# The order of score tiles at unit boundaries, and the join to the output projection, in a fused attention-times-gate kernel

## The chip, the cores and the metric

One core of one Trainium2 chip runs the whole kernel in one launch. The metric is the device time of that launch in microseconds (us), lower is better.

## What is computed

```python
xn = layernorm(x)                                    # x: 2048 x 512
q, k, v = split heads of (xn @ wqkv)                 # 32 heads of 16
o = softmax(q @ k.T * 16 ** -0.5) @ v                # per head, 2048 x 2048
s = o.reshape(2048, 512) @ wo
g = silu(gelu(xn @ w1 + b1) @ w2 + b2)               # hidden size 1376
out = x + s * g
```

All operands are float32. Products that need the precision are made of three matmuls on rounded high parts and remainders (`mm3`: high x high, high x low, low x high).

## The kernel before

The first stages (to about 437 us) make the layer norm, q, k, v and the gate g, and write q, k and g to DRAM. Among them the first 588 *score tiles* are already made (`SOON`). The rest, which the change touches, is the attention.

**Units and steps.** A unit is four heads by 512 queries; there are 32 (`NU`), and a unit takes 16 steps, one for each 128 keys. Steps are counted by n; `ua, ka = divmod(n, 16)` names the unit and the step in it, written (u, k) below. `L` is 512. A step is written out by hand as a string of letters, and each engine runs its own instructions in the order in which the letters issue them:

- **T** (`t_one`, L760): one *transposed tile*, 128 keys by 512 queries of one head, on half of the array's rows (contraction over 48 rows of q parts and 2 rows that hold the negated maxima, high and low). Four T make a step; the second and third share the two-bank tile `two`, the first writes a `ps` bank, the fourth `pst`. ScalarE turns them into exponentials (L763, L765): three ACTIVATEs a step.
- **S** (`s_whole`, L212): one *score tile*, 128 queries by 512 keys of one head, of which VectorE takes the maximum over keys (`s_max`, L218). Its only use is the row maximum that a later unit's T needs.
- **X, Y**: one score tile made in two halves of 256 columns, X on the upper rows and Y on the lower, with one maximum after Y. Y stands behind a no-op that waits until X is done. A step's usual string is `XTSTTYSTV` (three score tiles), or `TSTTSTV` (two).
- **V** (`pv_step`, L832): probabilities of the step before times v, with a column of ones for the denominator; four column tiles of 17 columns, accumulated over 16 steps in one PSUM bank. After the 16th, VectorE copies the bank out (`os`, L839).
- **H** (`w_halves`, L960): a quarter of one side of the output projection of two token tiles, six matmuls on half rows.
- **W** (`w_out`): gate and residual of a finished token tile, and its write to DRAM.

**Banks.** Score tiles rotate over three banks (`s_ring`). For units 1 to `FEW` the step (u, 1) makes two score tiles instead of three, and V changes its bank with the ring there. Units above `FEW` keep V's bank, so V of (u, 0), issued in step (u, 1), must wait for the copy of the unit before; there all steps make three score tiles, and step (u, 0) has the order `FIRST`.

**Maxima.** When a unit's 64 score tiles are done, `s_end0` reduces them to `nm`, `s_turn` transposes (L263) and splits them on GpSimd (`mh`, L265 and L266), and some steps later `s_send` writes them to DRAM (`mh_d`, L296; for the last unit two of the four writes come from GpSimd's queue, two from SyncE's). `load_mh` reads them back into the q tile's rows (L182) before the unit's first T.

**The join.** From step `DONE` on, no score tile is left. Steps then carry H, in the orders of `TWO` and `BOTH`, and two steps' V stand together in every second step. `gate` computes tanh on ScalarE (L894) and a product on VectorE (L895); `w_two` rounds two tiles of o to high parts on ScalarE (L938) and remainders on GpSimd (L941). `at(n, f, ...)` puts such helpers into step n, by default behind its fourth T (pos=3).

**The end.** After step 512 come the last six token tiles: three matmuls per k block (L107, in `mm3`), `w_gate` (L966), `w_add` (L971) and the write (L972). The last tile is done in two halves of 256 columns (`cols`).

Of the kernel before, what the change touches and what calls it, by code (L numbers as in the profile page):

```python
# [16 lines left out]
P = 128  # L17
S = 2048
D = 512
H = 32  # L20
DH = 16
KT = D // P
NT = S // P
# [11 lines left out]
NW = 10  # L35
EARLY = 4
AHEAD = ((-3, 0), (-3, 3), (-2, 0), (-2, 3))
DONE = 493
FILL0 = 2
APART = 5  # L40
HB = 5
DEALT = "00111111121112121112121112121112111211111212111212111212111212111211"
W2B = 2
ORDER = {0: "TTTTV", 2: "TSTTSTV", 3: "XTSTTYSTV"}
FIRST = "STXTTSYTV"
TWO = ("HTTTTHWV", "TTTTHHV")
BOTH = {DONE: "HHTTTTV", DONE + 3: "HHTTTTWV"}
SOON = 588
FEW = 16
SIDES = ((1, 1), (0, 0), (0, 1), (1, 0))  # L50
HC = CH // 2
PAIRED = 26
KB = 3
VP = (((0, 8),), ((0, 2), (1, 2)), ((2, 3),))
VB = (((0, 2), (1, 2)), ((1, 8),))
XB = 6
BANKS = ("ttvt", "xtmt", "ttvt")


@with_exitstack  # L60
def fused(ctx: ExitStack, tc: tile.TileContext, x, wqk, wv, wo, w1, b1, w2, out):
    nc = tc.nc
# [32 lines left out]
    def zip2(cols):  # L95
        return cols.rearrange("p (a b) -> p b a", a=2)

    def unzip(cols):
        return cols.rearrange("p (b a) -> p a b", a=2)
# [15 lines left out]
    NU = NG * NCH  # L115
# [71 lines left out]
    later, ended, errands, sent = [], [], [], set()  # L187

    def units_of(u):
        return (u,) if u >= PAIRED else (u - u % 2, u - u % 2 + 1)  # L190

    def tick():
        for e in later:
            e[0] -= 1

    def flush():
        while later and later[0][0] <= 0:
            u = later.pop(0)[1]
            s_send(u)
# [36 lines left out]
    def s_op(op):  # L236
        if op == "S":
            if whole:
                s_whole(whole.pop(), 1)
            else:  # L240
                whole.append(jobs.pop(0))
                s_whole(whole[0], 0)
        elif op == "X":
            if not cut:
                cut[:] = [jobs.pop(0), 0]
            ps, pool = s_tile(True)
            x = s_mm(ps, cut[0], 0, 0, cut[1] * HC, HC)
            cut[2:] = [ps, pool, x]
        else:
            job, n, ps, pool, x = cut  # L250
            hold = nc.tensor.nop().ins
            tc.add_manual_dep(hold, x.name, SYNC, reason="row tile done")
            s_mm(ps, job, 1, HC, n * HC, HC)
            s_max(ps, job, slice(0, 2), n)
            s_ring.append(pool)
            cut[1] += 1
            if n:
                cut.clear()

    def s_turn(u, nm):  # L260
        later.append([8 if u == NU - 1 else 12, u])
        nt = qring.tile([P, 2 * GH * NCH], F32, name="nt", bufs=1)
        nc.vector.transpose(nt, nm)  # L263
        mh = MH[u] = qring.tile([P, 2, 2 * GH * NCH], F32R, name="mh", bufs=1)
        nc.gpsimd.tensor_copy(mh[:, 0], nt)  # L265
        nc.gpsimd.tensor_sub(mh[:, 1], nt, mh[:, 0].bitcast(F32))  # L266

    def s_end0(u):
        ended.remove(u)
        us = units_of(u)  # L270
        w = u % 2 * GH * NCH
        nm = nms[u // 2 % 2]
        mx = MX.pop(u).rearrange("p a b c n -> p (a b) (c n)")
        nc.vector.tensor_reduce(nm[:, w:w + GH * NCH], mx, axis=AX.X, op=OP.max, negate=True)
        if u == us[-1]:
            if "seen" in prog or u == NU - 1:
                s_turn(us[0], nm)
            else:
                put_off.append((us[0], nm))
        del QS[u]  # L280
        if "seen" in prog:
            ask_qs(u + 2)
        else:
            load_qs(u + 2)
# [127 lines left out]
    with ExitStack() as s1:  # L412
# [36 lines left out]
        def norm(t):  # L449
            xns[t] = w1k.tile([P, D], F32, name="xn", bufs=4)  # L450
            nc.vector.tensor_scalar(xns[t], xs.pop(t), mv[:, t, 0:1], ve[:, 4, t:t + 1],
                                    op0=OP.subtract, op1=OP.mult)
            if t + XB < NT:
                load_x(t + XB)

# [50 lines left out]
        for k in range(KT):  # L506
            nc.sync.dma_start(wv_r[:, k], wv[:, k])
        for t in range(6, XB):
            load_x(t)
# [209 lines left out]
    def quad(n, at):  # L719
        us = first[n]  # L720
        for u, b in zip(us, BANKS[n]) if at == 0 else ():
            if b == "t":
# [99 lines left out]
    def pv_step(u, k):  # L822
        g = u // NCH
        if k == 0:
            if 0 < u <= FEW:
                s_ring.insert(1, v_home.pop())
# [88 lines left out]
        w_round([(t, k) for t in T3], ot[NCH - 1][:, k].rearrange("p (t s) -> p t s", s=P), lo)  # L915

    def cols(t):
        n = 2 if t == NT - 1 else 1
        return [slice(i * D // n, (i + 1) * D // n) for i in range(n)]

    def w_mul(t, ks, parts=(0, 1)):
        if t not in PW:
# [41 lines left out]
    def w_gate(t, i=0):  # L964
        gx, cs = GX[t], cols(t)[i]
        nc.vector.scalar_tensor_tensor(gx[:, 0, cs], PW[t][i][:, :cs.stop - cs.start], 0.5, gx[:, 0, cs],  # L966
                                       op0=OP.mult, op1=OP.mult)

    def w_add(t, eng, i=0):
        gx, cs = GX[t], cols(t)[i]  # L970
        eng.tensor_add(gx[:, 0, cs], gx[:, 0, cs], gx[:, 1, cs])  # L971
        (nc.gpsimd if t < NW else nc.sync).dma_start(out[t * P:(t + 1) * P, cs], gx[:, 0, cs])  # L972

    def w_out(t, eng):
        w_gate(t)
        w_add(t, eng)

    todo = {}

    def at(n, f, *a, pos=3):  # L980
        todo.setdefault((n, pos), []).append((f, a))
# [4 lines left out]
    def due(n):  # L986
        return min(4 * L, SOON + 3 * n - min(FEW, max(0, n - 1) // 16))

    for u in range(NU):
        g, c = divmod(u, NCH)  # L990
        if c == 0 and g == KB:
            for i in range(6):
                at(52 + i // 2, load_k, g, (i,), nc.gpsimd, 0, CH)
                at(56 + i // 2, load_k, g, (i,), nc.gpsimd, CH, CH)
                at(64 + i // 2, load_k, g, (i,), nc.gpsimd, S // 2, S // 2)
        elif c == 0 and g > KB:
            for i in range(6):
                at(64 * (g - KB + 1) + 6 + i, load_k, g, (i,), nc.gpsimd)
        if u >= 2:
            at(16 * u - 14, load_qt, u)  # L1000
            last = units_of(u)[-1]
            need = min(n for n in range(L) if due(n) >= 64 * (last + 1))
            need += 10 if u < PAIRED else 6 if u < NU - 1 else 2
            at(max(16 * u - 14, need), load_mh, u)
        if u < NU - 1:
            at(16 * u + 17, o_move, u, pos=0)
            at(16 * u + (25 if u < NU - 2 else 19), o_den, u, pos=0)
            at(16 * u + (27 if u < NU - 2 else 20), o_dn, u)
            at(16 * u + (31 if u < NU - 2 else 23), o_div, u, nc.gpsimd)
    T3 = range(NT - NCH, NT)  # L1010
    late = range(NW, NT)
    for t in range(NW):
        n = DONE + 4 * (t // 2)
        at(n - 3 + t % 2, load_gx, t)
        if t % 2 == 0:
            for i in range(2):
                at(n + i - 2 if t else n + 2 * i - 7, w_two, t, 2 * i)
            for i in range(4):
                for j in range(2):
                    at(n + i, w_halves, t, i % 2 * 2 + j, i // 2, pos="H")  # L1020
        at(n + t % 2, gate, t)
        at(n + 3, w_out, t, nc.gpsimd, pos="W")
    for i, t in enumerate(late):
        n = L - 2 * len(late) - 1 + 2 * i
# [10 lines left out]
    for n in range(L + 1):  # L1035
        ua, ka = divmod(n, 16)
        want = due(n) - due(n - 1)
        i = 0
        if put_off and ka > 1:
            s_turn(*put_off.pop(0))  # L1040
        else:
            for u in list(ended):
                if u >= PAIRED or ka > 2 and since.setdefault(u, n) < n:
                    s_end0(u)
        order = BOTH.get(n, TWO[n % 2]) if n >= DONE else ORDER[want] if n else ORDER[0]
        if want == 3 and ka == 0 and ua > FEW:
            order = FIRST
        for op in order:
            if op in "SXY":
                s_op(op)  # L1050
            elif op == "H":
                f, args = todo[n, "H"].pop(0)
                f(*args)
            elif op == "W":
                for f, args in todo.get((n, "W"), []):
                    f(*args)
            elif op == "V":
                for v in range(n - 1, n) if n < DONE else range(n - 2, n) if n % 2 == 0 else ():
                    if v >= 0:
                        pv_step(*divmod(v, 16))  # L1060
                for _ in range(4):
                    tick()
                flush()
            else:
                if EARLY <= 4 * n + i < 4 * L:
                    t_one(ua, ka, i, True)
                for f, args in todo.get((n, i), []):
                    f(*args)
                i += 1
# [17 lines left out]
    for t, i in [(t, i) for t in T3 for i in range(len(cols(t)))]:  # L1087
        w_mul(t, KS if t == NT - 1 else KS[2:] if t == T3[2] else KS[3:], (i,))
        w_gate(t, i)
        w_add(t, nc.vector, i)  # L1090


# [35 lines left out]
```

## Time and profile before

| what | value |
|---|---|
| median of 3 runs | 1495.87 us (1495.28 to 1495.96) |
| the profiled execution's own time | 1496.0 us |
| its span in the trace | 1494.2 us |
| steps of attention with score tiles | about 437 to 1418 us |
| steps with output projection | 1418 to 1473 us |
| last six token tiles | 1473 to 1494.2 us |

The trace is of one execution; its own time stands 0.1 us above the median, and its span 1.8 us below its own time. A timeline row gives the start in us, the length of what it merges, the engine, the line, the operation, output and input names, shape and count; in square brackets stands the idle time ahead of it on its engine and what ended it. PEld is TensorE's weight load, SPq a DMA issued by SyncE.

### The profile page before, as it was taken

Reading aid. Unit: us, or ns where it says so; the run is one execution under the profiler, and the core shown is the slowest. Engines: PE = TensorE matmul, PEld = TensorE weight load, DVE = VectorE, ACT = ScalarE, POOL = GpSimd, SP = SyncE. Lnnn points to the kernel's source line nnn. Section 1 sums busy time; section 2 is a strip of 40 time slices with the busy share of each in tenths; the row PEclk is TensorE's granted clock in tenths of the full one; section 3 lists DMA queues with packets and bytes.
Section 4 is the critical chain, followed back from the end, with each engine's and each line's share of the span. In section 5 each row is a group of like instructions: output and inputs, shape, how many; then the busy total and the mean of one; then the engine's idle time right before and its main releaser. Section 6 shows DMA issues by size and latency. Waiting matters only on the chain.

```text
span 1494.2 us, 31296 instructions
## 1 busy us (share of the span) xinstructions
PE 1487.4 (100%) x12234; PEld 870.5 (58%) x12234; DVE 1396.7 (93%) x2292; ACT 1202.8 (81%) x1884; POOL 358.9 (24%) x378
## 2 busy tenths in 40 slices
PE   9999999999999999999999999999999999999998
PEld 8899999999974444444444444444444444444456
DVE  8799999999999999999999999999999999999935
ACT  4333433434359999999999999999999999999994
POOL 4246666657540021011100200100010000000154
PEclk9999999999999999999999999999999999999999
DMA  6526354474341122114210511411141111110163
GB/s 212 160 74 175 105 158 128 147 167 139 118 126 27 34 51 42 41 49 68 53 30 22 86 31 34 73 31 33 34 70 31 35 31 34 42 31 20 51 209 118
DMA packets 78275, 116.57 MB, mean 78 GB/s; under 512 B 28180, under 2 KB 28436, under 8 KB 76952
## 3 DMA queue, kind: packets, MB, share of 16 engines
q1 hardware_dynamic: 73632, 99.27, 24.3%
q0 software_dynamic: 4144, 14.72, 5.1%
q8 instruction: 96, 1.57, 0.5%
q10 hardware_dynamic: 352, 0.59, 0.1%
q14 instruction: 51, 0.42, 0.1%
HBM read 84.09 MB, written 25.97 MB: 74 GB/s over the span
## 4 chain that ended last, share of the span: by engine, by line
PE 99%; DVE 1%; DMA 0%; ACT 0%; issue 0%; ACTq 0%
PE ps L832 27%; PE ps L212 19%; PE ps L623 10%; PE pst L760 8%; PE two L760 7%; PE pv L832 6%; PE ps L760 4%; PE sp L623 4%; PE pv L212 4%; PE pst L623 2%; PE pv L623 2%; PE ps L960 1%; PE pst L494 1%; PE ps L494 1%; PE pv L960 1%; PE pv L474 0%
## 5 line engine op out<-in xcount | busy, mean ns | idle before, releaser
L218 DVE TENSOR_REDUCE mx<-ps 128x2 f32<-128x512 f32 x1658 | 1077.1, 687 | 43.0 <-PE ps L212 17.1
L765 ACT ACTIVATE slot<-two 128x1024 f32<-128x1024 f32 x511 | 520.6, 1019 | 0.0
L832 PE MATMUL ps<-slot,vsb 128*17 128x512 f32 (+1 forms) x3328 | 436.3, 598 | 0.0
L763 ACT ACTIVATE slot<-ps 128x512 f32<-128x512 f32 x515 | 307.6, 597 | 13.6 <-PE ps L760 6.9
L763 ACT ACTIVATE slot<-pst 128x512 f32<-128x512 f32 x511 | 309.5, 606 | 0.0
L212 PE MATMUL ps<-kt,slot 48*128 48x256 f32 (+1 forms) x980 | 299.0, 361 | 0.0
L212 PEld LDWEIGHTS ps<-kt,slot 48*128 48x128 f32 x980 | 164.5, 184 | 219.6 <-DVE mx L218 211.2
L218 DVE TENSOR_REDUCE mx<-pv 128x2 f32<-128x512 f32 x390 | 266.6, 684 | 8.1 <-PE pv L212 1.0
L623 PE MATMUL ps<-slot,w1h 64*128 64x512 f32 x1088 | 201.6, 376 | 0.0
L212 PE MATMUL ps<-kt,qz 48*128 48x512 f32 x512 | 194.1, 379 | 0.0
L760 PE MATMUL two<-qt,kt 50*128 50x512 f32 x766 | 188.7, 379 | 0.4 <-ACT slot L765 0.4
L760 PE MATMUL ps<-qt,kt 50*128 50x512 f32 x387 | 184.3, 476 | 0.0
L760 PE MATMUL pst<-qt,kt 50*128 50x512 f32 x383 | 161.4, 422 | 0.0
L623 PEld LDWEIGHTS ps<-slot,w1h 64*128 64x128 f32 x1088 | 141.3, 186 | 13.0
L623 PE MATMUL ps<-slot,w1l 64*128 64x512 f32 x544 | 138.9, 376 | 0.0
L212 PE MATMUL pv<-kt,slot 48*128 48x256 f32 (+1 forms) x378 | 137.8, 365 | 0.0
L212 PE MATMUL ps<-slot,slot 48*128 48x256 f32 (+1 forms) x458 | 137.4, 361 | 0.0
L212 PEld LDWEIGHTS ps<-slot,slot 48*128 48x128 f32 x458 | 76.2, 184 | 95.7 <-DVE mx L218 92.1
L395 POOL TENSOR_TENSOR hl<-hg,hh 128x512 fp32r<-128x512 f32 x76 | 95.9, 1281 | 142.1 <-ACT hh L394 126.2
L377 ACT ACTIVATE hg<-ps,b_sb 128x512 f32<-128x512 f32 x44 | 27.9, 684 | 125.2 <-PE ps L623 117.9
L832 PEld LDWEIGHTS ps<-slot,vsb 128*17 128x17 f32 (+1 forms) x3328 | 56.8, 96 | 99.8 <-issue 96.1
L212 PEld LDWEIGHTS pv<-kt,slot 48*128 48x128 f32 x378 | 69.5, 184 | 77.5 <-DVE mx L218 74.6
(214 smaller groups left out, 2329.3 us busy)
## 6 DMA issues: line engine op xcount, KB each, us to landing
raw<-in_w SPq DMA_DIRECT2D x88, 256.0 KB
qk_h<-hh SPq DMA_DIRECT2D x32, 256.0 KB
qk_l<-hl SPq DMA_DIRECT2D x32, 256.0 KB
qt<-qk_h SPq DMA_DIRECT2D x128, 64.0 KB
slot<-qk_h SPq DMA_DIRECT2D x92, 64.0 KB
g_d<-hg POOLq DMA_DIRECT2D x16, 256.0 KB, 4.0
qt<-qk_l SPq DMA_DIRECT2D x64, 64.0 KB
dn<-den_d SPq DMA_DIRECT2D x32, 128.0 KB
```

The costliest lines, as they stand in the source:

```text
L212: return nc.tensor.matmul(ps[:, c0:c0 + w], QS[u][r, p, qi * P:(qi + 1) * P], zip2(kts[u // NCH % KB][p][r, k0:k0 + w]), start=True, stop= ...
L218: nc.vector.tensor_reduce(MX[u][:, 2 * p:2 * p + 2, qi, ki][:, heads, parts], ps.rearrange("p (n c) -> p n c", c=HC), axis=AX.X, op=OP.max)
L377: nc.scalar.activation(halves(raw), unzip(ph.pop(u)), AF.Gelu_apprx_tanh, bias=b1_sb[:, u[2]:u[2] + 1])
L395: nc.gpsimd.tensor_sub(hl, raw, hh.bitcast(F32))
L494: nc.tensor.matmul(ps, w, cols, start=n == s == k == 0, stop=n == 2 and k == KT - 1)
L623: i = nc.tensor.matmul(ps, lhs[r], rhs[r], start=first, stop=last).ins
L760: nc.tensor.matmul(ps, kts[g % KB][p][r, k * P:(k + 1) * P], zip2(QT[u][r, p, :]), start=True, stop=True)
L763: nc.scalar.activation(PT[u, k][:, 2 * p + a, :], ps, AF.Exp, scale=SCALE)
L765: nc.scalar.activation(PT[u, k][:, :2], TP["two"], AF.Exp, scale=SCALE)
L832: nc.tensor.matmul(PV[u][32 * j:32 * j + w, :], vsb.rearrange("p t w -> p (t w)")[:, k * H * VW + h:k * H * VW + h + w], PT[u, k][:, j, :] ...
L960: HALF[0] = nc.tensor.matmul(PW[i][0], OTS[i, k][x][r], zip2((wo_h, wo_l)[y][r, k]), start=k == 0 and side == 0 and n == 0, stop=k == KT - ...
```

## The change

Eight edits go together.

1. `FEW` 16 to 22: units 17 to 22 now change V's bank too and make two score tiles in their second step. Six score tiles are put off, which makes the score steps two more, and `DONE` goes from 493 to 495.
2. `FIRST` gets a second order, used in step (u, 1) of units above `FEW`: X, two T and Y ahead of the two whole S.
3. The first two projection steps carry four H each instead of two (`BOTH`), so that the 40 H fit 18 steps; `gate` of the first two tiles stays at steps 493 and 494, `w_two` of the next pair at 495 and 496.
4. `load_mh` of the last unit goes to M, behind the V of step 496; units 26 to 29 load one step later.
5. `s_turn`'s delay is 8 instead of 12 for unit 30.
6. `s_end0` is not run in the tenth step of a unit (k = 9), where the reciprocal of the denominators stands.
7. The last tile is cut at column 352 instead of 256.
8. Of its first part the residual is added on GpSimd, and of its second the write goes out from ScalarE's queue.

```diff
-DONE = 493
+DONE = 495
...
-FIRST = "STXTTSYTV"
+FIRST = ("STXTTSYTV", "XTTYSTSTV")
 TWO = ("HTTTTHWV", "TTTTHHV")
-BOTH = {DONE: "HHTTTTV", DONE + 3: "HHTTTTWV"}
+BOTH = {DONE: "HHTTTTHHV", DONE + 1: "HHHHVMTTTTW", DONE + 2: "HHTTTTV", DONE + 3: "HHTTTTWV"}
 SOON = 588
-FEW = 16
+FEW = 22
...
+LAST = 352
...
     def s_turn(u, nm):
-        later.append([8 if u == NU - 1 else 12, u])
+        later.append([8 if u >= NU - 2 else 12, u])
...
     def cols(t):
-        n = 2 if t == NT - 1 else 1
-        return [slice(i * D // n, (i + 1) * D // n) for i in range(n)]
+        return [slice(0, LAST), slice(LAST, D)] if t == NT - 1 else [slice(0, D)]
...
-        (nc.gpsimd if t < NW else nc.sync).dma_start(out[t * P:(t + 1) * P, cs], gx[:, 0, cs])
+        (nc.gpsimd if t < NW else nc.scalar if i else nc.sync).dma_start(out[t * P:(t + 1) * P, cs], gx[:, 0, cs])
...
-            need += 10 if u < PAIRED else 6 if u < NU - 1 else 2
-            at(max(16 * u - 14, need), load_mh, u)
+            need += 10 if u < PAIRED else 7 if u < NU - 2 else 6 if u < NU - 1 else 2
+            at(max(16 * u - 14, need), load_mh, u, pos=3 if u < NU - 1 else "M")
...
-        n = DONE + 4 * (t // 2)
+        n = DONE - 2 + 4 * (t // 2)
...
-                    at(n + i, w_halves, t, i % 2 * 2 + j, i // 2, pos="H")
+                    at(n + i if t else DONE + i // 2, w_halves, t, i % 2 * 2 + j, i // 2, pos="H")
...
+                if ka == 9 and u < NU - 2:
+                    continue
                 if u >= PAIRED or ka > 2 and since.setdefault(u, n) < n:
                     s_end0(u)
...
-        if want == 3 and ka == 0 and ua > FEW:
-            order = FIRST
+        if want == 3 and ka < 2 and ua > FEW:
+            order = FIRST[ka]
...
-        w_add(t, nc.vector, i)
+        w_add(t, nc.gpsimd if t == NT - 1 and i == 0 else nc.vector, i)
```

Line numbers below L57 are one higher after the change up to `cols`. TensorE in the second step of unit 23 (score tiles read `slot_4416`, 256 columns is X or Y; T reads `qt`; V reads `vsb`), before:

```order
L212 MATMUL pv<-kt_595,slot_4416 128x256
L760 MATMUL ps<-qt_6899,slot_4415 128x512
L212 MATMUL ps<-kt_595,slot_4416 128x512
L760 MATMUL two<-qt_6899,slot_4414 128x512 x2
L212 MATMUL pv<-kt_595,slot_4416 128x256
L212 MATMUL ps<-kt_595,slot_4416 128x512
L760 MATMUL pst<-qt_6899,slot_4415 128x512
L832 MATMUL ps<-slot_16770,vsb 32x512 x4
```

and after, the same step:

```order
L213 MATMUL pv<-kt_595,slot_4416 128x256
L761 MATMUL ps<-qt_6899,slot_4415 128x512
L761 MATMUL two<-qt_6899,slot_4414 128x512
L213 MATMUL pv<-kt_595,slot_4416 128x256
L213 MATMUL ps<-kt_595,slot_4416 128x512
L761 MATMUL two<-qt_6899,slot_4414 128x512
L213 MATMUL ps<-kt_595,slot_4416 128x512
L761 MATMUL pst<-qt_6899,slot_4415 128x512
L833 MATMUL ps<-slot_16728,vsb 32x512 x4
```

The halved tile is complete after the second T, ahead of both whole ones; the number of matmuls is the same.

VectorE at the join, from the last score tiles on (`mx` is a maximum of a score tile, `gx<-slot` the product of `gate`, `gx<-ps` that of `w_gate`), before:

```order
L218 TENSOR_REDUCE mx<-ps 128x2 x2
L218 TENSOR_REDUCE mx<-pv 128x2
L274 TENSOR_REDUCE nm_597<-mx 128x16
L263 STREAM_TRANSPOSE nt<-nm_597 128x32
L895 SCALAR_TENSOR_TENSOR gx<-slot_20192,gx 128x512 x2
L966 SCALAR_TENSOR_TENSOR gx<-ps,gx 128x512 x2
L839 COPY os<-ps 128x512
```

and after:

```order
L219 TENSOR_REDUCE mx<-ps 128x2 x2
L896 SCALAR_TENSOR_TENSOR gx<-slot_20153,gx 128x512
L219 TENSOR_REDUCE mx<-ps 128x2
L219 TENSOR_REDUCE mx<-pv 128x2
L219 TENSOR_REDUCE mx<-ps 128x2
L275 TENSOR_REDUCE nm_597<-mx 128x16
L264 STREAM_TRANSPOSE nt<-nm_597 128x32
L896 SCALAR_TENSOR_TENSOR gx<-slot_20153,gx 128x512
L840 COPY os<-ps 128x512
L966 SCALAR_TENSOR_TENSOR gx<-ps,gx 128x512
L966 SCALAR_TENSOR_TENSOR gx<-pv,gx 128x512
```

The first product of `gate` now stands ahead of the last three maxima, and the copy of unit 30's V ahead of `w_gate`.

GpSimd at the join (`mh` are the last unit's split maxima, `slot<-slot,dn` is a division of unit 29's o, `ol<-slot,oh` a remainder of `w_two`), before:

```order
L265 CAST mh<-nt 128x32
L266 TENSOR_TENSOR mh<-nt,mh 128x32
L296 DMA mh_d<-mh 16x2x32 x2
L871 TENSOR_TENSOR slot_6896<-slot_6896,dn 64x512
L941 TENSOR_TENSOR ol<-slot_6895,oh 128x512 x2
```

and after:

```order
L266 CAST mh<-nt 128x32
L267 TENSOR_TENSOR mh<-nt,mh 128x32
L872 TENSOR_TENSOR slot_6896<-slot_6896,dn 64x512
L941 TENSOR_TENSOR ol<-slot_6895,oh 128x512
L297 DMA mh_d<-mh 16x2x32 x2
L941 TENSOR_TENSOR ol<-slot_6895,oh 128x512
```

GpSimd's two writes of the maxima now stand behind the division and behind the first remainder.

More of the change, by code (lines that the diff above doesn't have):

```diff
@@ L1053, in fused @@
                 f(*args)
-            elif op == "W":
-                for f, args in todo.get((n, "W"), []):
+            elif op in "WM":
+                for f, args in todo.get((n, op), []):
                     f(*args)
```

## The prediction

> **What bounds the kernel now.** I read the page, then the windows by stage, then timelines of single engines at three places: a unit boundary, the join at step 493, and the end.
>
> ```profile
> 972.00:1418.00 446.00, 446.00 (x3560) 195.41 (x3558) 429.64 (x715) 440.10 (x669) 27.02 (x40) 1.00 0.16 37
> ```
>
> The row gives the stretch, its sum, and the busy time of TensorE, its weight loads, VectorE, ScalarE and GpSimd, each with a count. From 972 to 1418 us TensorE reads as full, VectorE is busy 96%, ScalarE 98.7%. TensorE's records include waiting matmuls, so the exponentials pace the score steps and score tiles come close behind. From 1418 on, H takes the place of S and VectorE has little to do. The copies of V's bank mark the units (VectorE, start in us):
>
> ```profile
> 468.58 0.68 DVE L839 COPY os<-pv 128x512 f32<-128x512 f32 x1
> 945.57 0.68 DVE L839 COPY os<-pv 128x512 f32<-128x512 f32 x1
> 977.22 0.68 DVE L839 COPY os<-ps 128x512 f32<-128x512 f32 x1
> 1169.58 0.68 DVE L839 COPY os<-ps 128x512 f32<-128x512 f32 x1
> ```
>
> These belong to units 0, 15, 16 and 22. Units 1 to 15, which change V's bank, take 476.99/15 = 31.80 us each; 17 to 22, which keep it, 192.36/6 = 32.06. A boundary with a kept bank costs 0.26 us. Where it goes, at unit 19:
>
> ```profile
> 1041.36 0.68 DVE L839 COPY os<-ps 128x512 f32<-128x512 f32 x1
> 1041.96 0.68 DVE L218 TENSOR_REDUCE mx<-pv 128x2 f32<-128x512 f32 x1
> 1042.56 1.95 DVE L218 TENSOR_REDUCE mx<-ps 128x2 f32<-128x512 f32 x3
> 1043.89 0.18 PEld L212 LDWEIGHTS ps<-slot,slot 48*128 48x128 f32 x1 [0.18 <-DVE mx L218]
> 1045.81 0.60 ACT L763 ACTIVATE slot<-ps 128x512 f32<-128x512 f32 x1 [0.19 <-PE ps L760]
> ```
>
> VectorE starts something every 0.60 us without a pause: the copy stands ahead of the second step's three maxima (the merged row holds two of them and the third step's first), the last of those ends at 1042.56 + 0.60 + 0.68 = 1043.84, and the second S of the third step (PEld at 1043.89) needs its bank. The T and V behind that S come late, and ScalarE idles 0.19 us.
>
> **The change part by part.** The sum is made against the profiled execution.
>
> (a) Six boundaries (units 17 to 22) become cheap ones: -6 x 0.26 = -1.6 us.
>
> (b) The new `FIRST` order for the eight that remain (23 to 30): 0. VectorE still does copy, halved tile, two whole tiles, in an unbroken chain; only the first two maxima change places. The S that stalls needs the fourth place of that chain, as before. TensorE gets to V of (u, 0) a little sooner, but that V needs the copy's end (1042.04; it starts at 1042.1 anyway). Bounds: -8 x 0.26 = -2.1 if the stall went, +0.9 if each boundary lost another 0.11 (a rival below).
>
> (c) Two more score steps. Two steps, V to V, took 1417.02 - 1413.05 = 3.97 us, so +3.97.
>
> ```profile
> 1413.05 1.05 PE L832 MATMUL ps<-slot,vsb 128*17 128x512 f32 x8
> 1417.02 1.05 PE L832 MATMUL ps<-slot,vsb 128*17 128x512 f32 x8
> 1418.00 0.48 PE L960 MATMUL ps<-wo_h,oh 64*128 64x512 f32 x2
> 1419.40 0.38 PE L760 MATMUL ps<-qt,kt 50*128 50x512 f32 x1
> 1419.84 0.38 PE L960 MATMUL ps<-wo_h,oh 64*128 64x512 f32 x2
> 1422.93 1.91 PE L832 MATMUL ps<-slot,vsb 128*17 128x512 f32 x16
> 1424.78 0.48 PE L760 MATMUL ps<-qt,kt 50*128 50x512 f32 x1
> 1425.31 0.38 PE L960 MATMUL ps<-wo_h,oh 64*128 64x512 f32 x2
> 1427.91 0.38 PE L760 MATMUL ps<-qt,kt 50*128 50x512 f32 x1
> 1428.43 1.91 PE L832 MATMUL ps<-slot,vsb 128*17 128x512 f32 x16
> 1417.90 0.60 ACT L763 ACTIVATE slot<-pst 128x512 f32<-128x512 f32 x1
> 1419.82 0.60 ACT L763 ACTIVATE slot<-ps 128x512 f32<-128x512 f32 x1 [1.32 <-PE ps L760]
> ```
>
> (d) Two projection steps fewer for the same 40 H. V pair to V pair is 5.50 us (1422.93 to 1428.43): four H are 2.60 (1425.31 to 1427.91), so two steps' T and V are 2.90: -2.9.
>
> (e) The old join lost time: HH 1.40 (1418.00 to 1419.40), T 0.44 (to 1419.84), H 0.65, T 0.44, H 0.65 make 3.58, but the V pair came at 1422.93, 4.93 after 1418.00. The 1.35 were T's waiting for ScalarE, which had idled 1.32 behind HH (1419.82). The new order has six H between step 495's T and 496's: -1.3.
>
> (f) `gate` of tile 0 stays at step 493, which is now a score step. Its product waits for the tanh, and the last three maxima stand behind it.
>
> ```profile
> 1421.22 0.60 ACT L763 ACTIVATE slot<-pst 128x512 f32<-128x512 f32 x1
> 1421.69 0.64 ACT L894 ACTIVATE slot<-gx 128x512 f32<-128x512 f32 x1
> 1422.37 0.69 DVE L895 SCALAR_TENSOR_TENSOR gx<-slot,gx 128x512 f32<-128x512 f32 x1 [3.23 <-ACT slot L894]
> ```
>
> On the clock of the trace, step 493's last exponential would start at 1417.90 + 1.97 = 1419.87, the tanh 0.47 later, the product 0.68 after that (1421.02), then two maxima at 0.60 each, the second done at 1422.93. H takes the banks of exactly these two tiles. It could start at 1418.00 + 3.97 = 1421.97 and starts at about 1423.0, which I call h: +1.0.
>
> (g) The last unit's maxima. GpSimd's two writes stand behind a remainder that waits for ScalarE's rounding, which stands behind step 495's exponentials.
>
> ```profile
> 1426.69 0.60 ACT L763 ACTIVATE slot<-pst 128x512 f32<-128x512 f32 x1
> 1427.17 0.64 ACT L938 ACTIVATE oh<-slot 128x512 fp32r<-128x512 f32 x1
> 1427.95 1.28 POOL L941 TENSOR_TENSOR ol<-slot,oh 128x512 fp32r<-128x512 f32 x1 [5.52 <-ACT oh L938]
> 1420.03 1.06 POOL L296 DMA_DIRECT2D mh_d<-mh  x2 [0.29 <-POOL mh L266]
> 1422.23 0.53 SPq L182 DMA_DIRECT2D qt<-mh_d  x2
> 1474.62 0.61 SPq L851 DMA_DIRECT2D dr<-os  x1
> 1476.55 0.25 DVE L859 RECIPROCAL dr<-dr 128x16 f32<-128x16 f32 x1 [3.13 <-DMA dr<-os]
> ```
>
> From h: HH 1.40, then T and 0.42 later its first exponential, the last 1.40 after that, rounding 0.48, remainder 0.78, its 1.28, the writes' issue 1.1, their landing 1.14 (1421.09 to 1422.23), load and landing 1.93 (1474.62 to 1476.55): 9.9, call it 10.0. TensorE reaches the last unit's first T after HH 1.40, T 0.44, six H 3.90, V pair 1.85: 7.6. Before, the load was issued 5.7 us ahead of that T (1427.91). So TensorE waits: +2.4. Behind that T stand all H and V that follow. Bounds: 0 if the writes land in time, +3 if loads of x and g, which SyncE now issues ahead of the maxima, are still moving.
>
> (h) Three steps' T (0.53 each in this stretch, 1424.78 to 1425.31) then stand between two V pairs with only four H: 4.2 us for TensorE, but ScalarE needs two full steps and two extras before the third T's bank is free (rounding, tanh: 2 x 1.98 + 2 x 0.5 = 5.0 after the first exponential's start, 0.5 behind the T), so the V pair comes after about 5.4: +1.2. Bounds +0.6 to +1.4.
>
> (i) The last tile. Rows of the warm-up and of the end:
>
> ```profile
> 4.80 3.74 PE L523 MATMUL pv<-vsb 128*128 128x128 f32 x32
> 1488.76 0.28 PE L107 MATMUL two<-wo_h,oh 128*128 128x256 f32 x1
> 1489.99 0.28 PE L107 MATMUL two<-wo_h,slot 128*128 128x256 f32 x1
> 1490.91 0.42 DVE L971 TENSOR_TENSOR slot<-slot 128x256 f32<-128x256 f32 x1
> 1477.48 2.16 DVE L971 TENSOR_TENSOR kt<-kt 128x512 f32<-128x512 f32 x1
> 1477.80 1.29 POOL L906 TENSOR_TENSOR ol<-ot,oh 128x512 fp32r<-128x512 f32 x1
> ```
>
> 256 columns start 0.112 apart (11 intervals in 1.23 us), and 128 columns, in the warm-up, also 0.112 (31 in 3.46). So 160 columns save TensorE nothing, while 352, at the 0.112 / 256 of the shorter ones or a little less each, cost up to 0.154: 12 x 0.042 = +0.5. The last product and add, 0.42 each at 256 columns, save at most 0.42 x 96 / 256 = 0.16 each at 160; I take 0.25 for both: +0.25. The Trainium skill weighs the same row in two ways. By the columns streamed (the Trainium skill, "TensorE: Matmul & The Clock Gate", Back-to-back issue gap: columns over 2.4 ns plus 2.5) a short product of 160 would start an estimated 69 ns after the last, and the item would be about -0.3. By the weight load (the Trainium skill, same page, LDWEIGHTS: 128 columns over 1.2, an estimated 107 ns whatever is streamed) 160 saves nothing; the trace's equal 0.112 for 128 and 256 speaks for this one.
>
> The add on VectorE at 1477.48 took 2.16 us with GpSimd at work at 1477.80: the first half's add, now on GpSimd, can so stretch the second half's add if they meet, by at most the first half's own length of about 0.9 (352 / 512 of 1.29), and only if it starts late. Bounds of (i): -0.3 (the 352 columns at no cost) to +0.9.
>
> (j) `s_end0` out of k = 9, the delays of units 26 to 30: 0 (bounds -0.3 to +0.3); these transfers have several steps of lead.
>
> Sum: -1.6 + 0 + 3.97 - 2.9 - 1.3 + 1.0 + 2.4 + 1.2 + 0.25 = +3.0. On 1496.0 that is 1499.0; the median stands 0.13 lower, so 1498.8. About 0.2%, 3.0 us, is what a measurement tells from no change: this forecast lies on that line.
>
> **The rivals.**
> - *The maxima are in time* (GpSimd's writes do not end last). For: the old slack was several us. Against: the queue order above. Then the second HH waits instead for `w_gate` behind the copy, about 0.9 us, and (h) stays 0.2 longer: 2.2 less, 1496.6.
> - *The new order clears the boundary stall*: -2.1, also 1496.7. For: whole tiles are asked for later. Against: the unbroken chain on VectorE.
> - *The join costs nothing*, (f), (g), (h) all 0, because H and T find other cover: 1498.8 - 4.6 = 1494.2; together with the rival above 1492.1.
>
> Rows for the fourth, of an old second step:
>
> ```profile
> 1041.13 0.37 PE L212 MATMUL ps<-slot,slot 48*128 48x256 f32 x1
> 1041.45 0.49 PE L760 MATMUL two<-qt,kt 50*128 50x512 f32 x2
> ```
>
> - *The new order costs* (the other side, slower): Y now stands one T closer to X, and its no-op waits for X. If X is not done by then, Y's weights load in the open and the step is about 0.11 longer (one interval above); ScalarE's first exponential has no slack there, 8 x 0.11 = +0.9: 1499.7. It decides where X needs longer than the two T between; in the rows X is recorded for 0.37 and the two T ahead of Y's place would start within 0.32 of X (1041.13 to 1041.45), so it is close.
>
> **How the numbers follow.** My case 0.48: down by 0.6 (h), 0.55 (i) and 0.3 (j) it reaches 1497.4, up by 0.6 (g), 0.2 (h), 0.65 (i), 0.3 (j) and part of (b) 1501.0; half of it lies above 1498.9. Maxima in time 0.18; stall cleared 0.09; join free 0.06, with the stall cleared 0.07; new order costs 0.12. Slower by over 0.2%: 0.24 + 0.12 = 0.36; faster, below 1492.9: 0.10 (the double case, and 0.03 where the last tile gains beside one of its two); the rest, 0.54, within. The range takes my case and the rivals down to the free join with the lower end of (i) and (j), 1494.2 - 0.8 = 1493.4, and leaves out the double case and the tails, about 0.15.
>
> **What the profile after would show.** Right: copies of units 16 and 22 some 190.8 us apart; the boundary stall of 0.18 on PEld unchanged for units 23 to 30; HH of step 495 waiting about 1 us for a maximum; the last unit's first T waiting about 2.4 us for a DMA; last adds at the end not earlier. Wrong: no DMA wait at that T (g falls), boundaries under 31.9 us after unit 22 (b falls), V pairs at the join under 5 us apart (h falls).

## The result, and the profile after

The changed kernel takes 1504.7 us (median; 1504.28 to 1505.2) beside 1495.91 for the kernel before: ratio 1.0059, 95% interval 1.0046 to 1.0072. The forecast was 1498.8, with a range up to 1501.0: the sign was right, the size was not, by 5.9 us. By stretches of the two traces (spans 1494.2 and 1502.9 us; V(n) is the start of step n's V on TensorE, which is issued in a later step; the last column places the prediction's terms: (a), (b), (c) to (f), (g) with (h), and (i)):

| stretch | before | after | difference | forecast |
|---|---|---|---|---|
| copies of units 16 to 22 (boundaries 17 to 22) | 192.36 | 190.59 | -1.77 | -1.6 |
| copies of units 22 to 29 (new `FIRST` order) | 224.65 | 225.12 | +0.47 | 0 |
| copy of unit 29 to V(494) | 34.20 | 35.01 | +0.81 | +0.3 |
| V(494) to V(496) | 5.50 | 10.05 | +4.55 | +4.15 |
| V(496) to V(510) | 38.09 | 38.09 | 0 | 0 |
| V(510) to the end | 22.16 | 26.78 | +4.62 | +0.25 |

The copies that the first two rows rest on (timeline of VectorE, after; the last row is the kernel before's unit 29, not shown yet):

```profile
977.26 0.68 DVE L840 COPY os<-ps 128x512 f32<-128x512 f32 x1
1167.85 0.68 DVE L840 COPY os<-ps 128x512 f32<-128x512 f32 x1
1392.97 0.68 DVE L840 COPY os<-ps 128x512 f32<-128x512 f32 x1
```

```profile
1394.23 0.68 DVE L839 COPY os<-ps 128x512 f32<-128x512 f32 x1
```

The pair of V that begins with V(510), before and then after (TensorE; the spans end at 1494.2 and 1502.9):

```profile
1472.02 1.91 PE L832 MATMUL ps<-slot,vsb 128*17 128x512 f32 x16
```

```profile
1476.12 1.91 PE L833 MATMUL ps<-slot,vsb 128*17 128x512 f32 x16
```

The join, after (timelines of TensorE, GpSimd and SyncE's queue):

```profile
1421.33 0.45 PE L960 MATMUL ps<-wo_h,oh 64*128 64x512 f32 x1 [0.47 <-DVE mx L219]
...
1427.98 1.91 PE L833 MATMUL ps<-slot,vsb 128*17 128x512 f32 x16
1431.59 0.45 PE L761 MATMUL ps<-qt,kt 50*128 50x512 f32 x1 [1.71 <-DMA qt<-mh_d]
...
1426.31 1.28 POOL L941 TENSOR_TENSOR ol<-slot,oh 128x512 fp32r<-128x512 f32 x1 [0.95 <-ACT oh L938]
1427.54 1.06 POOL L297 DMA_DIRECT2D mh_d<-mh  x2
...
1429.73 0.53 SPq L183 DMA_DIRECT2D qt<-mh_d  x2
```

The first H waits 0.47 us for a maximum; the last unit's first T waits 1.71 for the maxima, whose two last writes GpSimd issues at 1427.54, behind the remainder (1426.31). Both are where the forecast had them. What it had not is in the windows right behind: TensorE's granted clock (third column from the end) is 0.50 from 1432 to 1435.4.

```profile
1428.00:1432.00 4.00, 2.29 (x21) 0.69 (x21) 1.89 (x3) 0.00 (x0) 0.60 (x2) 1.00 0.03 7
1432.00:1435.40 3.40, 3.40 (x19) 3.20 (x20) 0.00 (x0) 2.52 (x4) 0.66 (x1) 0.50 0.29 49
```

And at the end, after: GpSimd's add of the first part, and the closing DRAINs of GpSimd and SyncE (columns: count, then shortest, median and longest in ns, then first and last start):

```profile
1494.71 0.93 POOL L971 TENSOR_TENSOR slot<-slot 128x352 f32<-128x352 f32 x1 [9.21 <-DVE slot L966]
1495.51 0.32 DVE L971 TENSOR_TENSOR slot<-slot 128x160 f32<-128x160 f32 x1
...
L1126 POOLq DRAIN  x3: 46/102/7430, 1494.7 to 1502.6; - x3
L1126 SPq DRAIN  x3: 7/7/13, 1498.1 to 1502.4; - x3
```

The same of the kernel before, with GpSimd's last operation:

```profile
1479.90 1.48 POOL L906 TENSOR_TENSOR ol<-ot,oh 128x512 fp32r<-128x512 f32 x1 [0.82 <-ACT oh L905]
...
L1124 POOLq DRAIN  x3: 46/102/7983, 1479.9 to 1493.9; - x3
L1124 SPq DRAIN  x3: 7/7/13, 1493.3 to 1493.7; - x3
```

GpSimd's first closing DRAIN runs from 1494.7 for 7.43 us, to 1502.1, which is 6.46 after its add's end (1495.64). SyncE has seen every write land at 1498.1, and its last closing step comes 4 us later, after GpSimd's DRAIN. In the kernel before the same DRAIN started at 1479.9 and ended at 1487.85, again 6.46 after GpSimd's last operation (1481.38), and 5.5 us ahead of SyncE's: it cost nothing. The row was there before; the forecast had not read it.

### The profile page after: what moved, and what is told of

It reads as the page before. It is cut to its first block, busy times and chain, and to the rows that moved or that the text cites. A ratio compares the mean times of both kernels' runs of the same rounds, so it can differ in the third digit from the quotient of the medians.

```text
span 1502.9 us, 31302 instructions
## 1 busy us (share of the span) xinstructions
PE 1490.6 (99%) x12230; PEld 874.3 (58%) x12230; DVE 1398.6 (93%) x2291; ACT 1204.4 (80%) x1884; POOL 360.3 (24%) x379
## 4 chain that ended last, share of the span: by engine, by line
PE 97%; DMA 1%; ACT 1%; DVE 1%; POOL 1%; issue 0%; DVEq 0%; ACTq 0%; POOLq 0%; SPq 0%
PE ps L833 25%; PE ps L213 18%; PE ps L624 10%; PE pv L833 8%; PE pst L761 8%; PE two L761 7%; PE ps L761 4%; PE sp L624 4%; PE pv L213 4%; PE pst L624 2%; PE pv L624 2%; PE ps L960 1%; PE pst L495 1%; PE ps L495 1%; PE pv L960 0%; PE pv L475 0%
## 5 line engine op out<-in xcount | busy, mean ns | idle before, releaser
L219 DVE TENSOR_REDUCE mx<-ps 128x2 f32<-128x512 f32 x1690 | 1096.8, 687 | 43.7 <-PE ps L213 17.0
L833 PE MATMUL ps<-slot,vsb 128*17 128x512 f32 (+1 forms) x3072 | 402.7, 598 | 0.0
L213 PE MATMUL ps<-kt,slot 48*128 48x512 f32 (+1 forms) x979 | 302.2, 363 | 0.0
L219 DVE TENSOR_REDUCE mx<-pv 128x2 f32<-128x512 f32 x358 | 245.3, 685 | 8.7
L213 PE MATMUL ps<-slot,slot 48*128 48x512 f32 (+1 forms) x480 | 140.9, 361 | 0.0
L213 PEld LDWEIGHTS ps<-slot,slot 48*128 48x128 f32 x480 | 79.3, 184 | 101.2 <-DVE mx L219 97.7
L833 PE MATMUL pv<-slot,vsb 128*17 128x512 f32 (+1 forms) x1024 | 134.8, 598 | 0.0
```

The source lines that it names most:

```text
L213: return nc.tensor.matmul(ps[:, c0:c0 + w], QS[u][r, p, qi * P:(qi + 1) * P], zip2(kts[u // NCH % KB][p][r, k0:k0 + w]), start=True, stop= ...
L219: nc.vector.tensor_reduce(MX[u][:, 2 * p:2 * p + 2, qi, ki][:, heads, parts], ps.rearrange("p (n c) -> p n c", c=HC), axis=AX.X, op=OP.max)
L833: nc.tensor.matmul(PV[u][32 * j:32 * j + w, :], vsb.rearrange("p t w -> p (t w)")[:, k * H * VW + h:k * H * VW + h + w], PT[u, k][:, j, :] ...
```

## Experiments

Differences of a few tenths are read from the traces; the medians carry 0.1% (1.5 us). Runs without an interval are single executions.

**GpSimd's closing DRAIN: take the late add away, or add it to the kernel before.**

```diff
-        w_add(t, nc.gpsimd if t == NT - 1 and i == 0 else nc.vector, i)
+        w_add(t, nc.vector, i)
```

> The changed kernel, with the last tile's first add on VectorE again; the cut at 352 and the write from ScalarE's queue stay. Theory (drain): GpSimd's closing DRAIN ends 6.46 us after its last operation, in both traces (1481.38 to 1487.85 before, 1495.64 to 1502.11 after). Before, that was over long ahead of the end. Without the late add the end is set by the last write again, so about 3.9 us less: near 1500.8. Rival (cut and queues): the uneven cut or the write from the other queue makes the end late; then 0 to 0.5 us less, 1504.2 to 1504.7.

Measured 1499.83 us, ratio to before 1.0027 (1.0017 to 1.0038): 4.9 less than the changed kernel, 1.0 more than forecast. From V(510) to the end 22.18 us, against 26.78 and, before, 22.16.

The reverse edit in the kernel before:

> The kernel before, with one edit: the add of the last tile's first half on GpSimd (cut at 256, both writes from SyncE, as before). Drain theory: the add ends near 1490.8 on that trace's clock, the DRAIN 6.46 later, 1497.3, against 1493.4 for SyncE's last wait: about +3.9, near 1499.8. Rival (cut and queues): no change, 1495.9, or +0.3 for a write that GpSimd's longer add holds up.

Measured 1500.11, ratio 1.0028 (1.0017 to 1.0039): +4.2, forecast +3.9. The edit is enough by itself, and without it the end is back at the old length: shown from both sides. The cut and the queue, the rival, are worth nothing (22.18 with them, 22.16 without; a load that varies from execution to execution, told below, took 4.1 us in both).

Two more runs of the kernel before ask what starts the 6.46 us: a copy of a single column, and a DMA issue without computation.

```diff
+            tiny = wb.tile([P, 1], F32, name="tiny", bufs=1)
+            nc.gpsimd.tensor_copy(tiny, GX[t][:, 0, :1])
```

> The kernel before, with one more operation: GpSimd copies one column (128x1) of the last tile after the first half's add; nobody reads it. Theory (a fixed time from GpSimd's last operation to the end of its DRAIN, whatever the operation): the copy ends near 1490.8, the DRAIN 6.46 later at 1497.2, the time 1499.5 to 1499.9, as with the whole add. Rival (the DRAIN waits for the add's size, or for its write): below 1497.

```diff
-        (nc.gpsimd if t < NW else nc.sync).dma_start(...)
+        (nc.gpsimd if t < NW or i else nc.sync).dma_start(...)
```

> The kernel before, with the write of the last tile's second half issued by GpSimd; no computation on GpSimd at the end. If the 6.46 us follow any instruction of GpSimd, a DMA issue too: issue at 1491.36 to 1491.9, DRAIN to 1498.4, the time near 1501. If they follow computations alone: the slower issue and landing only (0.56 and 2.3 us against 0.33 and 1.4), near 1497.

Measured 1500.52 and 1501.37, 0.6 above the range given for the copy and 0.4 above the figure for the write; the DRAIN's length is what was forecast. GpSimd's last instruction and its DRAIN, of the copy and then of the write:

```profile
1490.97 0.19 POOL L1093 COPY tiny<-slot 128x1 f32<-128x1 f32 x1 [9.66 <-DVE slot L971]
...
L1127 POOLq DRAIN  x3: 46/102/6673, 1491.0 to 1498.1; - x3
```

```profile
1491.40 0.56 POOL L972 DMA_DIRECT2D out<-slot  x1 [10.31 <-DVE slot L971]
...
L1124 POOLq DRAIN  x3: 46/102/7110, 1491.4 to 1499.0; - x3
```

The copy ends at 1491.16, the DRAIN 6.67 after 1490.95, at 1497.62: 6.46 later. The write's issue ends at 1491.96, the DRAIN at 1498.49: 6.53. The time does not depend on the size of the operation, nor on whether it computes. It does depend on something else: over all the runs it is 6.30 us where the program issues 76 DMAs from GpSimd (the writes of the maxima moved to SyncE, below), 6.46 with 78, and 6.53 with the 79 of the run with the write. Two runs of the changed kernel cut that count far from the end; the first moves 18 loads of k, the second these and 30 more.

```diff
-                at(52 + i // 2, load_k, g, (i,), nc.gpsimd, 0, CH)
+                at(52 + i // 2, load_k, g, (i,), nc.sync, 0, CH)
...
-                at(64 * (g - KB + 1) + 6 + i, load_k, g, (i,), nc.gpsimd)
+                at(64 * (g - KB + 1) + 6 + i, load_k, g, (i,), nc.sync)
```

> The changed kernel, late add and all, with 18 loads of k near 540 us issued by SyncE instead of GpSimd; nothing near the end is touched. In thirteen traces the DRAIN's 6.30, 6.46 and 6.53 us go with 76, 78 and 79 DMAs issued by GpSimd in the whole program: 0.083 us each. Theory (the DRAIN's length is 0.083 us times that count): 60 are left, 4.97 us, so the DRAIN ends 1.5 earlier and the time is near 1503.2. Rival (a fixed 6.3 us and a little for the last DMAs): 6.3 to 6.46, 1504.5 to 1504.7.

> As the run before it, with all 48 loads of k from 540 us on issued by SyncE. Theory: 30 DMAs of GpSimd are left, the DRAIN takes 2.49 us and ends no later than SyncE's own wait for the last write, so the late add costs nothing any more: near 1500.7, if the loads disturb nothing from SyncE. Rival (fixed): 1504.5 to 1504.7.

Measured 1502.99 (ratio 1.0042, 1.0025 to 1.0059) and 1500.08 (1.0025, 1.0015 to 1.0035). GpSimd's add, its DRAIN and SyncE's in the second:

```profile
1493.98 0.93 POOL L971 TENSOR_TENSOR slot<-slot 128x352 f32<-128x352 f32 x1 [9.33 <-DVE slot L966]
...
L1126 POOLq DRAIN  x3: 46/93/3508, 1493.9 to 1498.0; - x3
L1126 SPq DRAIN  x3: 7/7/13, 1497.3 to 1497.7; - x3
```

From the add's end the DRAIN takes 5.00 us with 60 DMAs and 2.54 with 30 (forecast 4.97 and 2.49), and with 30 it ends 0.1 us behind SyncE's wait: the late add is nearly free (1500.08 beside 1499.83 without it; the two times are 0.2 and 0.6 under the forecasts). The length is 0.083 to 0.085 us for each DMA that GpSimd has issued in the whole program, 62 of the 78 more than 400 us earlier. The size of a DMA does not count: two writes of 4 KB less take off 0.16 us, 18 loads of 64 and 128 KB 1.46, 30 more of 128 and 256 KB 2.46, each time some 0.08 a DMA. What the DRAIN does for each of them stays open.

**The wait for the maxima, and the clock behind it.**

```diff
-            eng = nc.gpsimd if u == NU - 1 and b % 2 else nc.sync
+            eng = nc.sync
```

> The changed kernel, with all four writes of the last unit's maxima from SyncE's queue, so that none stands behind GpSimd's division and remainder. Theory (wait and clock): the 1.71 us DMA wait at the last unit's first T goes, and with it the half clock of 3.41 us behind it (1.7 us of TensorE's time), though ScalarE then paces part of what follows: 2.6 to 3.4 us less, 1501.3 to 1502.1. Rival (the wait alone, the slow matmuls behind it having another cause): 1.7 less, 1503.0, with H still 0.43 apart near 1433. Second rival: the writes take as long from one queue, no change.

Measured 1502.76 (ratio 1.0047, 1.0031 to 1.0064), 1.9 less: by the time, the rival's number. In the trace the T's wait is gone and the granted clock is 1.00, as the theory had it, but V(494) to V(496) is 7.83 us, not the 6.6 to 7.4 that 2.6 to 3.4 less would leave: two waits that had lain under the long one are now in the open (waits of TensorE, 1420 to 1440 us):

```profile
PE ps L960 <- POOL ol L941: 0.6, 1, 0.6
PE ps L960 <- DVE gx L966: 0.6, 1, 0.6
PE ps L960 <- DVE mx L219: 0.5, 1, 0.5
```

H waits 0.6 for a remainder of `w_two` and 0.6 for the bank that `w_gate` reads, which stands behind V's copy.

The clock alone: the wait stays, and TensorE works through it.

```diff
             elif op in "WM":
                 ...
+                if op == "M":
+                    fill = ps_t.tile([P, CH], F32, name="pst")
+                    for _ in range(8):
+                        nc.tensor.matmul(fill, OTS[0, 3][0], zip2(wo_h[:, 3]), start=True, stop=True)
```

> The changed kernel, with eight matmuls of 128 rows and 512 columns, whose result nobody reads, between the last V pair and the last unit's first T: the wait for the DMA stays, but TensorE works through it. Theory (clock): the granted clock stays at 1.00 and H keeps its 0.215 spacing, about 1.0 to 1.7 us less, 1503.0 to 1503.7, although work was added. Rival (H is slow near 1433 for another reason, such as transfers under way): 1504.7 or up to 0.3 more.

Measured 1504.88: no gain, the rival's number again, and the trace says why. The same window as above:

```profile
1432.00:1435.40 3.40, 3.36 (x24) 2.40 (x24) 0.02 (x1) 2.90 (x6) 0.30 (x1) 1.00 0.23 49
...
1436.41 0.48 PE L960 MATMUL ps<-wo_h,ol 64*128 64x512 f32 x2 [0.65 <-POOL ol L941]
```

The clock stays at 1.00 and H runs 0.215 apart instead of 0.43. But H then waits 0.65 us for the remainder that slow matmuls had given time to: from the T to V(496) it is 5.99 us against 6.44, and the T itself comes 0.15 later behind the filler. What the clock costs here is 0.3 to 0.45 us, too little for these medians.

That it was the filler which kept the clock is not shown. Five traces have the wait (1.70 to 1.81 us) without a filler: four show the half clock behind it, the run with 18 loads of k on SyncE does not:

```profile
1431.81 0.45 PE L761 MATMUL ps<-qt,kt 50*128 50x512 f32 x1 [1.80 <-DMA qt<-mh_d]
...
1432.00:1435.40 3.40, 3.36 (x24) 2.29 (x23) 0.00 (x0) 3.04 (x6) 0.44 (x1) 1.00 0.32 53
```

The half clock begins at a time of its own, 0.43 us after that T in the changed kernel's trace, 0.98, 1.64 and 0.77 after it in the three others; T to V(496) took 6.44, 5.98, 6.23 and 6.04 there and 5.96 in the fifth, so it costs between nothing and 0.5. In the clock records of all these traces the clock changes only whole multiples of 3.413 us after its first rise to 1.00 (418 of them, 1426.77 us, in the four). In the four the whole wait lies between two such instants; in the fifth one falls at 1431.65, into the wait, and parts it into 1.64 and 0.16. In the run with the filler one falls at 1430.27, 0.2 us into the gap, so the clock may have stayed at 1.00 without the filler too. No trace without this wait shows a half clock in this stretch: the wait is part of the cause, and as far as five traces can tell it counts where it falls.

**The join: gates where ScalarE waits, and w_out ahead of V.** Both runs have the add on VectorE and the writes on SyncE.

```diff
-        at(n + t % 2, gate, t)
+        at(n + t % 2 if t > 1 else DONE, gate, t)
```

> The changed kernel with the add on VectorE and the four writes on SyncE (the two earlier edits together), and the gates of tiles 0 and 1 moved to step 495, where ScalarE waits for the last unit's T anyway. Theory (the gates in score steps cost twice, on ScalarE and as the product ahead of the maxima): the first H of step 495 no longer waits 0.47 us for a maximum, and two tanh (0.48 and 0.52) leave the paced steps; the V pair of step 496 comes 1.0 to 1.5 us earlier, the last unit's maxima some 1.6 earlier. Against 1499.83 - 1.94 = 1497.9 for the two edits alone: 1496.4 to 1496.9. Rival (what is won there is given back before the next V pair, since ScalarE paces the steps after): the V pair of step 498 less than 0.5 earlier, 1497.4 to 1497.9.

Measured 1496.74 in one execution, as the theory had it. The first H starts 0.98 behind the last V, without a wait:

```profile
1419.56 1.05 PE L833 MATMUL ps<-slot,vsb 128*17 128x512 f32 x8
1420.54 0.48 PE L960 MATMUL ps<-wo_h,oh 64*128 64x512 f32 x1
```

V(493) to V(494) falls from 8.17 to 7.13; V(494) to V(496) stays at 7.84, so nothing is given back.

```diff
-..., DONE + 1: "HHHHVMTTTTW", ...
+..., DONE + 1: "HHHHWVMTTTT", ...
...
-                at(n + i - 2 if t else n + 2 * i - 7, w_two, t, 2 * i)
+                if t == 2 and i:
+                    todo[DONE + 1, "W"].insert(0, (w_two, (t, 2 * i)))
+                else:
+                    at(n + i - 2 if t else n + 2 * i - 7, w_two, t, 2 * i)
```

> As the run with the gates in step 495, and in step 496 the second half of the next two tiles' rounding and w_out of tiles 0 and 1 ahead of V, not behind the last T. Theory (behind the DMA wait two waits lay hidden: H for the remainder, 0.59, and H for the bank that w_gate reads behind the copy, 0.56): both go, the distance from the V pair of step 496 to that of step 498 falls from 7.83 to 6.7 to 7.0, and the time to 1495.3 to 1496.0. Rival (ScalarE's exponentials pace this stretch anyway): 7.4 or more, 1496.3 or more.

```profile
1427.07 1.91 PE L833 MATMUL ps<-slot,vsb 128*17 128x512 f32 x16
1433.85 1.92 PE L833 MATMUL ps<-slot,vsb 128*32 128x512 f32 x16
```

V(494) to V(496) is 6.78, the waits are gone: the step behaves as expected. The time, 1496.41 (ratio 1.0003, 0.9993 to 1.0012), misses the forecast by 0.4. In the profiled execution V(510) to the end took 23.11 us against 22.35 in the run with the gates in step 495, all of it in one load, told below (4.81 us against 4.04); but that execution's own time, 1496.82, is 0.4 above the median, so the load does not explain the median's miss, which stays open.

**The second step's order.**

```diff
-FIRST = ("STXTTSYTV", "XTTYSTSTV")
+FIRST = ("STXTTSYTV", "XTSTTYSTV")
```

> The changed kernel, with the usual string XTSTTYSTV in the second step of units 23 to 30. Read in the trace by the copies of units 22 and 29 (seven units): 224.65 us before, 225.12 changed. Theory (the new order costs): back to 224.6 to 224.7, some 0.5 us less in all. Rival (the later reduction at k = 9 or the shifted loads cost it): 225.1 as now.

The copies of units 22 and 29:

```profile
1168.08 0.68 DVE L840 COPY os<-ps 128x512 f32<-128x512 f32 x1
1392.57 0.68 DVE L840 COPY os<-ps 128x512 f32<-128x512 f32 x1
```

224.49 us for units 23 to 29, against 225.12 with the new order and 224.65 before the change: the order alone costs all of the 0.47. The time of this one execution was 1503.85.

**All costs away.** The join's edits, the writes, the add and the old order together:

> As the run before it, with the usual string in the second step of units 23 to 30: 0.5 us less than that run, 1494.8 to 1495.5. If all theories hold, this is the changed kernel with its cheap boundaries and without its four new costs (GpSimd's late add, the late writes, the waits at the join, the new order), and stands 0.4 to 1.1 below the kernel before (1495.95). Rival: some cost of the join is still there, 1496 or more.

Measured 1495.35 beside 1496.08, ratio 0.9994 (0.9985 to 1.0003). With the old end (cut at 256, both writes from SyncE):

> The kernel with all four costs taken away (gates in step 495, writes on SyncE, w_out ahead of V, usual string in the second step, adds on VectorE), with the end of the kernel before: cut at 256, both writes from SyncE. The cut moves the time between V(510) and the end by 0.02 (22.18 against 22.16 us in the two traces that differ in it alone in that stretch), so the same as with the cut at 352: 1495.2 to 1495.5 beside the kernel before's 1496.0. Rival (the cut is worth its 0.25): 0.2 to 0.3 less than that run, 1495.1.

Measured 1495.57 beside 1496.13, 0.9996 (0.9987 to 1.0005): the cut makes no difference that shows.

> As the kernel with all four costs taken away and the cut at 352, except that two of the last unit's four writes go from GpSimd's queue again: the division of unit 29's o moves two steps later and both roundings of the next two tiles into step 496, so that the writes stand first on GpSimd. In the five traces with all four writes on SyncE, the write of the last denominators takes 2.43 us from its issue to the load that waits for it, in the others 2.1, and the time from V(510) to the end is 0.5 to 0.7 longer in those without GpSimd's late add. Theory (the two more DMAs on SyncE's queue cost it): 2.1 again, from V(510) to the end 22.2 to 22.3 against 22.75, the time 0.5 below the 1495.35 of that kernel: near 1494.9, 1.0 below the kernel before. Rival (chance of an execution, or another edit): 2.4, and 1495.3.

Measured 1495.63 beside 1496.4, 0.9995 (0.9986 to 1.0004): half right; the end had been 0.2 to 0.9 longer in the four traces that the expectation speaks of, not 0.5 to 0.7. SyncE's rows with all writes on SyncE, and then in this run:

```profile
1475.99 0.32 SPq L861 DMA_DIRECT2D den_d<-dr  x1
1478.42 0.59 SPq L866 DMA_DIRECT2D dn<-den_d  x1
```

```profile
1475.83 0.32 SPq L861 DMA_DIRECT2D den_d<-dr  x1
1477.91 0.58 SPq L866 DMA_DIRECT2D dn<-den_d  x1
```

The write of the denominators is back from 2.43 to 2.08 us, but the load behind it took 4.63 from issue to use, and the end is 22.71 after V(510), hardly better than 22.75. That load took 4.09 in the trace of before and 4.43 in that of after; in three runs of the kernel before with another end it took 3.90, 4.16 and 4.51 with the same instructions ahead of it, so it varies from execution to execution; why stays open. The three versions are thus 0.04 to 0.06% below the kernel before in their medians, each with an interval that includes no difference. They stand clearly below the changed kernel; that they beat the kernel before is not shown.

## Why the prediction was wrong, point by point

- **The step that failed is (i), the last tile.** It priced the add on GpSimd by its own length and by what it could do to VectorE's add, -0.3 to +0.9 with the cut, and did not ask what else follows GpSimd's last instruction. The program ends when every engine has drained, GpSimd's DRAIN takes 6.46 us with the 78 DMAs that it has issued, and the edit moved its start from 10 us ahead of the last VectorE operation to beside it: +4.6 for the stretch, of which 0.35 is the load above. Without that edit the changed kernel runs in 1499.83, inside the range and 1.0 from the forecast; that it is so near is in part luck, since errors of (g), (h) and the clock cancel in good part, below. The other parts of (i) were near: 352 columns start 0.149 apart (forecast 0.154), 160 columns 0.111, and the cut as a whole is worth 0.02, not 0.25.
- **(a)** -1.77 for -1.6: right.
- **(b)** 0 was wrong: the rival on the slower side came true, in sign. At the second step of unit 24 (the first exponentials of the second and the third step on ScalarE, then a weight load of TensorE), before:

```profile
1201.91 0.60 ACT L763 ACTIVATE slot<-ps 128x512 f32<-128x512 f32 x1
1203.87 0.60 ACT L763 ACTIVATE slot<-ps 128x512 f32<-128x512 f32 x1
...
1204.14 0.18 PEld L212 LDWEIGHTS pv<-kt,slot 48*128 48x128 f32 x1 [0.18 <-DVE mx L218]
```

  and after:

```profile
1200.26 0.60 ACT L764 ACTIVATE slot<-ps 128x512 f32<-128x512 f32 x1
1202.49 0.60 ACT L764 ACTIVATE slot<-ps 128x512 f32<-128x512 f32 x1
...
1200.23 0.18 PEld L213 LDWEIGHTS pv<-kt,slot 48*128 48x128 f32 x1 [0.20 <-issue]
```

  The third step's stall of 0.18 is gone, and the second step is 2.23 long instead of 1.96: Y's no-op leaves the weight load idle for 0.20, the S and T behind Y are late, and ScalarE with them. Net 0.07 a unit, less than the 0.11 of the rival, on the same side. The stall's rival did not come true with it: that S still starts 0.05 us after the fourth operation of VectorE's chain ends (1204.09 before, 1202.53 after), 2.52 us behind the copy before and 2.63 after. VectorE's chain is as the forecast had it; S is only asked for later, since the step ahead of it is longer.
- **(c) to (e), and (f):** V(494) came 0.8 later against unit 29's copy, forecast 0.3. The first H waited 0.47 for the maximum where 1.0 was expected, but the late maxima cost more than this: the first H ran alone on its half of the rows for 0.5 us (1421.33, the other half from 1421.84). Moving the gates takes both away and gave back 1.04 in this stretch, so (f) as a cause was right in kind and size. Even then the first H is 6.15 ahead of V(494), where the forecast's clean sequence of H had 5.74; the four H of step 496 start 0.2 late with and without the gates there.
- **(g)** +1.71 for +2.4: right in mechanism and place; counted from the first H, the maxima came after 10.3 us (forecast 10.0), but TensorE was ready for that T after 8.6 (forecast 7.6). What the step left out is that TensorE's clock can fall behind such a wait: to 0.50 for 3.4 us behind 1.71 here. It cost up to 0.5 here and less in other runs, since a later wait for `w_two`'s remainder takes part of the time either way.
- **(h)** V(494) to V(496) without (g) is 7.83, forecast 1.85 + 5.4 = 7.25: 0.6 too little. The forecast had 1.2 in it for ScalarE's pace. The trace has two waits of 0.6 instead, one for GpSimd's remainder and one for `w_gate` behind V's copy (the forecast named the second, in a rival, at 0.9), and with both gone, and a rounding moved out of the stretch, it is 6.78. So the order of `w_two` and `w_gate` sets a good part of this stretch, not the exponentials alone. That V(494) to V(496) as a whole came out at +4.55 for +4.15 is luck in part: (g) 0.7 too large, (h) 0.6 too small and the clock's 0.45 left out cancel to 0.4.
- **(j)** 0: right. With the usual string in the second step the copies of units 22 to 29 are 224.49 apart, before the change 224.65, so the other edits there cost nothing that shows.

## What to carry to other kernels

Read the closing instructions of every engine (the last source line's rows) before moving work to the end: an engine that finishes early may hide a drain of several us, and the first operation put late on it costs whatever of that then stands out behind the other engines, however small the operation; here the cure is fewer DMAs from GpSimd, or nothing of GpSimd in the last 6 us. A long wait hides shorter ones behind it: before pricing its removal, list what the next instructions wait for, and move producers into the idle time that it leaves on the other engines, as the gates here. And an order that takes a stall from one step is only worth what it does not add to the step before; read two steps together.

## What the runs showed of the hardware

- GpSimd's closing DRAIN ends 0.083 to 0.085 us times the number of DMAs that it has issued behind its last instruction: 2.54 us with 30, 5.00 with 60, 6.30 with 76, 6.46 with 78, 6.53 with 79. An add of 352 or 256 columns and a copy of one made no difference. The Trainium skill ("VectorE: DVE Perf Modes", The DRAIN you can't avoid) speaks of closing DRAINs of about 12 ns on all engines; SyncE's 7 to 13 ns here, with over 1000 DMAs issued, agree with that; the first closing DRAINs of TensorE, VectorE and ScalarE end within 0.2 us of their engine's last work; GpSimd's does not agree.
- A wait of 1.70 to 1.81 us without a matmul, behind a pair of V, brought the granted clock to 0.50 for 3.41 us in four traces of five; in the fifth, with 1.80 us, it stayed at 1.00. The Trainium skill ("TensorE: Matmul & The Clock Gate", What's actually happening) tells of free-running windows of 3.4 us and of a half clock after an idle one: the length and the free-running windows agree, but here less than a whole window of idle time was enough.
- The 0.47 us wait at 1421.33 left the clock at 1.00.
